# Second MLP product: five of seven block products in 512-column matmuls, six rotating PSUM banks per pair, half of the weight sums made by adding transfers

## The chip, the cores and the metric

The kernel runs on one core of one Trainium2 chip. The metric is the device time of one execution in microseconds; the median of three runs of the kernel before is 534.46 us (534.25 to 535.26).

## The reference

One transformer-like block on x of shape (2048 tokens, 512 channels), in fp32: linear attention with a softmax feature map (32 heads of 16) with its residual, giving h, and then a token-mixing MLP over h. The change is in the last product of the MLP:

```python
h2 = h + B(layernorm(h))
# B: layernorm again, then
u = gelu(einsum("bsd,sf->bdf", h, w1) + b1)     # F = 1792
y = einsum("bdf,fs->bds", u, w2) + b2           # back to S = 2048 tokens
return y.transpose                              # (S, D)
```

So the output rows of token t are h[t] plus the sum over f of w2[f, t] x u[:, f] plus b2[t].

## The kernel before, in words

A product of two fp32 matrices is made of three TensorE matmuls in float32r: each operand is split into a high part (a rounding copy by ScalarE) and a remainder (a subtraction), and high x high, high x remainder and remainder x high are added up in PSUM. `split` (L55 to L58) makes the two parts: the copy at L57 on ScalarE, the subtraction at L58 on the engine that is passed.

The first MLP product (`fill`, L622 to L635, with `mm3`, L60 to L64) runs 512-column matmuls; it fills PSUM tiles `pu`, and `gelu` (L723) writes u.

The second product (L763 to L847) takes the 1792 = 7 x 256 rows of w2 and the 2048 = 8 x 256 tokens in blocks of 256 x 256, and multiplies a block by a 2 x 2 scheme with seven block products in place of eight (Strassen's in Winograd's form). `operands_u` (L729) makes the seven combinations of u, each 128 x 256, once per p and keeps high part and remainder side by side in `UB[p, m]` (tiles `un` for p = 0 and 1, `uf` for the others). `STEPS` (L763) is 8 pairs of token tiles (sp) x 7 row blocks (p) = 56 steps. For every two steps (`GRP`), that is 28 groups, `stream_w2` (L767 to L781)

- loads four 128 x 128 blocks for each step into `wraw`, of which there are three, by two transfers of 256 KB on SP's queue (L773);
- makes the three further combinations, and one in place, by four VectorE operations of 256 columns (L777 to L780);
- splits all seven into `whi` and `wlo`, of which there are two each (L57 on ScalarE and L58 on VectorE, 1792 columns).

`product` (L787) runs three matmuls of 256 columns, L789: weights `whi` with the high part of u, `whi` with its remainder, `wlo` with the high part. `PROD` (L784) lists the seven products with the bank and the half of the bank that each adds into: seven halves of four banks per pair of token tiles. Even pairs use the four banks of `ps_b`, odd ones those of `ps_f` and `ps_q` (L806). The last step of a pair goes bank by bank (L813, L818); in the last pair the last two steps do (L834), so that the banks end one after the other.

A pair is drained by one ScalarE copy (L820), three VectorE sums (L821 to L823) and two operations of 512 columns that add b2 as well (L825). The result goes to the output, which holds h already, by two transfers of 256 KB that add in memory, issued by GpSimd (L827). The last pair has loaded its rows of h ahead (L832) and adds on VectorE (L836 to L846), then stores (L844, L847).

The order on the engines: up to the first product's middle it is written out by hand; in the stage of the second product a planner decides it from its own estimate of the times. It keeps program order as the priority, takes what is ready, and fixes the order of each engine's queue, which then runs in order on the chip. `issue_after` (L776) keeps the VectorE sums behind one instruction of the first product. A tile with n buffers is written again only when all readers of its earlier use are done.

Of the kernel before, what the change touches and what calls it, by code (L numbers as in the profile page):

```python
# [9 lines left out]
F32 = mybir.dt.float32  # L10
F32R = mybir.dt.float32r
AF = mybir.ActivationFunctionType
ALU = mybir.AluOpType
# [4 lines left out]
P = 128  # L18
S, D, H, DH, F = 2048, 512, 32, 16, 1792
NT = S // P  # L20
KD = D // P
NF = F // P
NG = 8
# [10 lines left out]
def block_kernel(ctx: ExitStack, tc: tile.TileContext, x, xT, wT, phic, wo, w1, b1, w2, b2,  # L34
                 kvmask, ident_in, out):
    nc = tc.nc
# [9 lines left out]
    b2s = cst.tile([P, NT], F32, name="b2s")  # L46
# [21 lines left out]
    ps_q = ctx.enter_context(tc.tile_pool(name="ps_q", bufs=2, space=PSUM, side="right"))  # L68
# [290 lines left out]
    q = {"mm": 0, "logits": 0, "exp": 0, "sum": 0}  # L359
# [39 lines left out]
    for t in range(3, NT - 1):  # L399
        if t + 2 < NT:  # L400
            raw = load_x(t + 2)
# [193 lines left out]
    w2v = w2.rearrange("(k p) s -> p k s", p=P)  # L595
# [114 lines left out]
    NP = NF // 2  # L710
    HD = D // 2
# [9 lines left out]
    U, UB, far = {}, {}, {}  # L721
# [42 lines left out]
    GRP = 2  # L764
    AW = {}

    def stream_w2(n):  # L767
        steps = STEPS[n:n + GRP]
        raw = ws.tile([P, GRP, 7, P], F32, name="wraw", bufs=3)
        wh_ = ws.tile([P, GRP, 7, P], F32R, name="whi")  # L770
        wl_ = ws.tile([P, GRP, 7, P], F32R, name="wlo")
        for i, (sp, p) in enumerate(steps):
            nc.sync.dma_start(raw[:, i, 0:4].rearrange("p (k i) s -> p k (i s)", k=2),  # L773
                              w2v[:, 2 * p:2 * p + 2, sp * 2 * P:(sp + 1) * 2 * P])
            AW[sp, p] = wh_[:, i], wl_[:, i]
        with tc.issue_after(LO[-18]):  # L776
            nc.vector.tensor_add(raw[:, :, 4], raw[:, :, 0], raw[:, :, 2])  # L777
            nc.vector.tensor_sub(raw[:, :, 0], raw[:, :, 1], raw[:, :, 0])
            nc.vector.tensor_sub(raw[:, :, 5], raw[:, :, 4], raw[:, :, 1])
            nc.vector.tensor_sub(raw[:, :, 6], raw[:, :, 3], raw[:, :, 5])  # L780
# [6 lines left out]
    def product(o, a, b, start, stop):  # L787
        for i, (x, y) in enumerate(((0, 0), (0, 1), (1, 0))):
            nc.tensor.matmul(o, a[x], b[:, y], start=start and i == 0, stop=stop and i == 2, skip_group_check=True)  # L789

    def products(sp, ps, order):
        for a, b, bk, half, opens in order:
            for p in ps:
                wh_, wl_ = AW[sp, p]
                product(bank[bk][:, half], (wh_[:, a], wl_[:, a]), UB[p, b], p == 0 and opens, p == NP - 1)

    def flat(a):
        return a.rearrange("p k d -> p (k d)")

    for n, (sp, p) in enumerate(STEPS):  # L800
# [12 lines left out]
        by_bank = sorted(PROD, key=lambda m: m[2:4])  # L813
# [3 lines left out]
        if not last:  # L817
            products(sp, [p], by_bank)  # L818
            ot = uo.tile([P, 2, 2, HD], F32, name="ot", bufs=1)
            nc.scalar.activation(e[:, 1], bank[0][:, 0], AF.Copy)  # L820
            nc.vector.tensor_add(u2, bank[0][:, 1], e[:, 1])  # L821
            nc.vector.tensor_add(u3, bank[1][:, 0], u2)
            nc.vector.tensor_add(e[:, 0], bank[2][:, 0], u2)  # L823
            for i, add in enumerate((u3.unsqueeze(1).to_broadcast([P, 2, HD]), e)):
                nc.vector.scalar_tensor_tensor(ot[:, i], bank[2 + i], b2s[:, t + i:t + i + 1], add,  # L825
                                               op0=ALU.add, op1=ALU.add)
                nc.gpsimd.dma_start(out[(t + i) * P:(t + i + 1) * P, :], flat(ot[:, i]), accum_op=ALU.add)  # L827
            continue
# [5 lines left out]
        products(sp, [p - 1, p], by_bank)  # L834
        nc.scalar.activation(e[:, 1], bank[0][:, 0], AF.Copy)
        nc.vector.tensor_add(hb[1][:, 1], bank[0][:, 0], hb[1][:, 1])  # L836
        nc.vector.tensor_add(u2, bank[0][:, 1], e[:, 1])
        nc.vector.tensor_add(hb[1][:, 0], u2, hb[1][:, 0])
        nc.vector.tensor_add(u3, bank[1][:, 0], u2)
        nc.vector.tensor_add(hb[0], hb[0], u3.unsqueeze(1).to_broadcast([P, 2, HD]))  # L840
        nc.vector.tensor_add(hb[0][:, 0], bank[2][:, 0], hb[0][:, 0])
        nc.vector.tensor_add(hb[1][:, 0], bank[2][:, 0], hb[1][:, 0])
        nc.vector.tensor_add(hb[0][:, 1], bank[2][:, 1], hb[0][:, 1])
        nc.sync.dma_start(out[t * P:(t + 1) * P, :], flat(hb[0]))  # L844
        for k, q in ((0, nc.scalar), (1, nc.sync)):
            nc.vector.tensor_add(hb[1][:, k], bank[3][:, k], hb[1][:, k])  # L846
            q.dma_start(out[(t + 1) * P:NT * P, k * HD:(k + 1) * HD], hb[1][:, k])  # L847


def _layout(A_x, A_wqkv, A_w_phi, A_wo, B_w1, B_b1, B_w2, B_b2):  # L850
# [7 lines left out]
    for a in range(P // DH):  # L858
# [3 lines left out]

    wo = np.asarray(A_wo).reshape(2, 4, 2, 32, D).transpose(2, 0, 1, 3, 4).reshape(D, D)
# [8 lines left out]
        "w2": np.asarray(B_w2),  # L872
# [22 lines left out]
```

## Time and profile before

| what | value |
|---|---|
| median of three runs | 534.46 us |
| span of the profiled execution, first to last instruction | 532.6 us |
| TensorE busy in the span | 520.8 us (98%), 3616 matmuls |
| VectorE, ScalarE, GpSimd busy | 384.4, 271.9, 234.8 us |
| second product, first to last matmul start | 385.8 to 526.8 us |
| its matmuls | 1176 of 256 columns |
| 256 KB weight load, issue to landing, median in the stage | 3.2 us |
| 256 KB adding transfer to the output, issue to landing, median | 4.8 us |

The profile has no time of its own for the execution it recorded beside the span; what lies around the span is not in it, and the median of the runs is 1.9 us above it. Times in rows of instructions are microseconds from the span's start. PE is TensorE's matmul side, PEld its weight loads, DVE VectorE, ACT ScalarE, POOL GpSimd, SP the queue that issues plain transfers. In a row of instructions the first number is the start, the second the time busy, and `x8` the number of instructions merged into the row; matmuls overlap in the pipeline, so their rate is read from their starts. What stands after `<-` in brackets ended the idle time before the row. A row of a window has the window, then busy time and count for PE, PEld, DVE, ACT and POOL, the granted clock, the busy share of the DMA engines and GB/s.

### The profile page before, as it was taken

The numbers are of one execution on the slowest core, as the hardware profiler recorded it, in microseconds if no ns is written. First come the engines' busy times: TensorE is split into PE (matmuls) and PEld (weight loads), VectorE is DVE, ScalarE is ACT, GpSimd is POOL, SyncE is SP. The second block draws the span as 40 slices with busy tenths as digits, with TensorE's granted clock in tenths as the row PEclk, the third lists the DMA queues.
The fourth block names the chain that finished last, engine by engine and source line by source line (L and its number), as shares of the span: only waits on it lengthen the run. The fifth ranks groups of instructions, "written<-read, shape, count | busy, mean of one in ns | idle before, by whom it ended". The sixth has DMA issues, their size and how long they took to land.

```text
span 532.6 us, 9386 instructions
## 1 busy us (share of the span) xinstructions
PE 520.8 (98%) x3616; PEld 448.7 (84%) x3616; DVE 384.4 (72%) x680; ACT 271.9 (51%) x460; POOL 234.8 (44%) x190
## 2 busy tenths in 40 slices
PE   8999999999999989999999999999999999999995
PEld 7888888886877767777788888888899999999995
DVE  6993999877699989875325524835668877887784
ACT  6998844424336776557746423525444243343340
POOL 2589699877889988887325000000001101100110
PEclk9999999999999999999999999999999999999999
DMA  8633310020502233334255333542014556535631
GB/s 309 206 110 118 99 22 21 1 72 9 160 0 79 82 101 116 104 116 136 85 176 159 98 100 98 159 117 82 20 41 107 143 148 153 123 120 136 143 75 46
DMA packets 45486, 55.81 MB, mean 105 GB/s; under 512 B 3969, under 2 KB 33025, under 8 KB 45441
## 3 DMA queue, kind: packets, MB, share of 16 engines
q1 hardware_dynamic: 43136, 51.38, 30.7%
q0 software_dynamic: 2016, 3.67, 5.5%
q8 instruction: 28, 0.46, 0.4%
q10 hardware_dynamic: 288, 0.17, 0.1%
q14 instruction: 18, 0.14, 0.1%
HBM read 46.81 MB, written 8.39 MB: 104 GB/s over the span
## 4 chain that ended last, share of the span: by engine, by line
PE 83%; POOL 9%; DVE 3%; ACT 2%; issue 1%; DVEq 0%; POOLq 0%; ACTq 0%
PE py L789 26%; PE pu L62 11%; PE pu L63 11%; PE pu L64 11%; POOL ez L442 4%; POOL eq L460 3%; PE pv L63 2%; PE pv L64 2%; PE pv L62 2%; PE pk_ps L62 2%; PE pk_ps L63 2%; PE pk_ps L64 2%; POOL hs L58 2%; PE po L62 1%; PE kvp L207 1%; PE po L63 1%
## 5 line engine op out<-in xcount | busy, mean ns | idle before, releaser
L827 POOL DMA_DIRECT2D out<-ot x14 | 12.5, 1001 | 212.2 <-DVE ot L825 212.2
L789 PE MATMUL py<-uf,whi 128*128 128x256 f32 x560 | 96.2, 283 | 0.0
L63 PE MATMUL pu<-hs,whi 128*128 128x512 f32 x224 | 87.6, 391 | 1.8 <-POOL hs L58 1.8
L602 DVE TENSOR_TENSOR wlo<-wraw,whi 128x512 fp32r<-128x512 f32 x56 | 50.3, 903 | 51.8 <-ACT whi L610 50.7
L57 ACT ACTIVATE whi<-wraw 128x1792 fp32r<-128x1792 f32 x28 | 47.7, 1705 | 77.9 <-PE py L789 73.8
L62 PE MATMUL pu<-hs,whi 128*128 128x512 f32 x224 | 87.4, 395 | 0.0
L64 PE MATMUL pu<-hs,wlo 128*128 128x512 f32 x224 | 87.2, 390 | 0.0
L789 PEld LDWEIGHTS py<-uf,whi 128*128 128x128 f32 x560 | 83.3, 192 | 0.0
L789 PE MATMUL py<-uf,wlo 128*128 128x256 f32 x280 | 69.9, 283 | 0.0
L58 DVE TENSOR_TENSOR wlo<-wraw,whi 128x1792 fp32r<-128x1792 f32 x28 | 56.6, 2022 | 15.4 <-ACT whi L57 15.4
L610 ACT ACTIVATE whi<-wraw 128x512 fp32r<-128x512 f32 x56 | 35.0, 627 | 47.0 <-PE pu L63 44.8
L63 PEld LDWEIGHTS pu<-hs,whi 128*128 128x128 f32 x224 | 42.1, 188 | 11.0 <-POOL hs L58 2.8
L62 PEld LDWEIGHTS pu<-hs,whi 128*128 128x128 f32 x224 | 42.0, 188 | 10.9 <-issue 2.5
L64 PEld LDWEIGHTS pu<-hs,wlo 128*128 128x128 f32 x224 | 42.0, 188 | 9.1 <-DVE wlo L602 0.4
L789 PEld LDWEIGHTS py<-uf,wlo 128*128 128x128 f32 x280 | 49.7, 192 | 0.0
L442 POOL TENSOR_TENSOR ez<-eq,zB 128x1024 f32<-128x1024 f32 x16 | 40.9, 2559 | 2.5 <-ACT zB L488 2.5
L789 PE MATMUL py<-un,whi 128*128 128x256 f32 x224 | 38.4, 283 | 0.0
L195 POOL TENSOR_TENSOR pk<-pk,sk 128x1024 f32<-128x1024 f32 x16 | 31.0, 1941 | 9.8 <-DVE sk L194 9.0
L460 POOL TENSOR_TENSOR eq<-eq,w 128x1024 f32<-128x1024 f32 x16 | 32.0, 1997 | 4.0 <-DVE w L457 4.0
L789 PEld LDWEIGHTS py<-un,whi 128*128 128x128 f32 x224 | 33.2, 192 | 0.1
L199 POOL TENSOR_TENSOR zacc<-zacc,pk 128x1024 f32<-128x1024 f32 x13 | 31.3, 2405 | 0.6
L58 POOL TENSOR_TENSOR hs<-hn,hs 128x512 fp32r<-128x512 f32 x16 | 21.4, 1340 | 17.5 <-ACT hs L57 15.6
(165 smaller groups left out, 1176.5 us busy)
## 6 DMA issues: line engine op xcount, KB each, us to landing
wraw<-in_w SPq DMA_DIRECT2D x112, 256.0 KB, 2.9
xraw<-in_xT SPq DMA_DIRECT2D x16, 256.0 KB, 3.1
xh<-in_x SPq DMA_DIRECT2D x16, 256.0 KB, 2.6
h<-in_x SPq DMA_DIRECT2D x16, 256.0 KB, 2.7
out<-h SPq DMA_DIRECT2D x16, 256.0 KB, 3.0
out<-ot POOLq DMA_DIRECT2D x14, 256.0 KB, 4.8
wraw<-in_wT SPq DMA_DIRECT2D x12, 256.0 KB, 5.0
wo<-in_wo SPq DMA_DIRECT2D x4, 256.0 KB, 3.6
```

The lines of the kernel that those rows point to most:

```text
L57: nc.scalar.activation(hi, src, AF.Copy)
L58: lo_engine.tensor_sub(lo, src, hi)
L62: nc.tensor.matmul(o, ah, bh, start=first, stop=False)
L63: nc.tensor.matmul(o, ah, bl, start=False, stop=False)
L64: nc.tensor.matmul(o, al, bh, start=False, stop=last)
L195: nc.gpsimd.tensor_mul(heads(PK[t]), heads(PK[t]), sk.unsqueeze(2).to_broadcast([P, 2 * H, DH]))
L199: nc.gpsimd.tensor_add(zacc, zacc, PK[t])
L442: nc.gpsimd.tensor_mul(EZ[t], EQ[t], zB)
L460: nc.gpsimd.tensor_mul(heads(EQ[t]), heads(EQ[t]), W[t].rearrange("p g c h -> p (g c h)").unsqueeze(2).to_broadcast([P, 2 * H, DH]))
L602: LO.append(nc.vector.tensor_sub(wl_, raw, wh_).ins)
L610: nc.scalar.activation(wh_, raw, AF.Copy)
L789: nc.tensor.matmul(o, a[x], b[:, y], start=start and i == 0, stop=stop and i == 2, skip_group_check=True)
```

## The change

- w2 is laid out on the host so that a group's four blocks lie together: [28, 128, 4, 256]. A group is loaded by one transfer of 512 KB and a second of 128 KB that puts the first block into slot 4 as well; then one transfer of 256 KB issued by GpSimd adds the second block onto slot 0 and the third onto slot 4. VectorE makes two sums per group in place of four. `wraw` has four buffers in place of three.
- The sums differ in sign from those before, so the draining subtracts in places.
- Five of the seven products have a bank of their own: one matmul of 512 columns (`whi` with the high part and the remainder of u side by side, into both halves) and one of 256 (`wlo` with the high part, into the first half). The two halves are added when the bank is drained. The other two products share a bank, one half each, in three matmuls as before. In the last pair (`LAST`) the last product is in three as well.
- A pair takes six banks, which rotate over all eight.
- In every pair the last two steps go together, product by product.
- The scratch memory for the descriptors of GpSimd's transfers is 8192 bytes in place of the default.

```diff
     def stream_w2(n):
-        steps = STEPS[n:n + GRP]
-        raw = ws.tile([P, GRP, 7, P], F32, name="wraw", bufs=3)
-        wh_ = ws.tile([P, GRP, 7, P], F32R, name="whi")
-        wl_ = ws.tile([P, GRP, 7, P], F32R, name="wlo")
-        for i, (sp, p) in enumerate(steps):
-            nc.sync.dma_start(raw[:, i, 0:4].rearrange("p (k i) s -> p k (i s)", k=2),
-                              w2v[:, 2 * p:2 * p + 2, sp * 2 * P:(sp + 1) * 2 * P])
-            AW[sp, p] = wh_[:, i], wl_[:, i]
+        g = n // GRP
+        raw = ws.tile([P, 7, GRP * P], F32, name="wraw", bufs=4)
+        wh_ = ws.tile([P, 7, GRP * P], F32R, name="whi")
+        wl_ = ws.tile([P, 7, GRP * P], F32R, name="wlo")
+        nc.sync.dma_start(raw[:, 0:4], w2[g])
+        nc.sync.dma_start(raw[:, 4], w2[g, :, 0])
+        nc.gpsimd.dma_start(raw[:, 0:5:4], w2[g, :, 1:3], accum_op=ALU.add)
+        for i, step in enumerate(STEPS[n:n + GRP]):
+            AW[step] = wh_[:, :, i * P:(i + 1) * P], wl_[:, :, i * P:(i + 1) * P]
         with tc.issue_after(LO[-18]):
-            nc.vector.tensor_add(raw[:, :, 4], raw[:, :, 0], raw[:, :, 2])
-            nc.vector.tensor_sub(raw[:, :, 0], raw[:, :, 1], raw[:, :, 0])
-            nc.vector.tensor_sub(raw[:, :, 5], raw[:, :, 4], raw[:, :, 1])
-            nc.vector.tensor_sub(raw[:, :, 6], raw[:, :, 3], raw[:, :, 5])
+            nc.vector.tensor_add(raw[:, 5], raw[:, 4], raw[:, 1])
+            nc.vector.tensor_add(raw[:, 6], raw[:, 3], raw[:, 5])
         split(wh_, wl_, raw, nc.vector)
...
-    PROD = ((1, 1, 0, 0, True), (2, 6, 2, 1, True), (3, 3, 3, 1, True), (4, 4, 2, 0, False), (0, 0, 1, 0, True),
-            (5, 5, 0, 1, False), (6, 2, 3, 0, False))
+    PROD = ((1, 1, 0, None), (5, 5, 1, None), (0, 0, 2, 0), (4, 4, 2, 1), (2, 6, 3, None), (6, 2, 4, None),
+            (3, 3, 5, None))
+    LAST = PROD[:-1] + ((3, 3, 5, 0),)
...
+        if half is None:
+            nc.tensor.matmul(o, a[0], b, start=start, stop=stop, skip_group_check=True)
+            nc.tensor.matmul(o[:, 0], a[1], b[:, 0], start=False, stop=stop, skip_group_check=True)
+            return
         for i, (x, y) in enumerate(((0, 0), (0, 1), (1, 0))):
...
-            pools = [ps_f, ps_f, ps_q, ps_q] if sp % 2 else [ps_b] * 4
-            bank = [pool.tile([P, 2, HD], F32, name="py", tag="pu") for pool in pools]
-        if p < NP - 1 - last:
-            products(sp, [p], PROD)
+            bank = []
+            for _ in range(6):
+                pool = (ps_f, ps_q, ps_b, ps_b)[n_bank % 8 // 2]
+                bank.append(pool.tile([P, 2, HD], F32, name="py", tag="pu"))
+                n_bank += 1
+        order = LAST if last else PROD
+        if p < NP - 2:
+            products(sp, [p], order)
             continue
         if p < NP - 1:
             continue
+        products(sp, [p - 1, p], order)
...
             nc.scalar.activation(e[:, 1], bank[0][:, 0], AF.Copy)
-            nc.vector.tensor_add(u2, bank[0][:, 1], e[:, 1])
-            nc.vector.tensor_add(u3, bank[1][:, 0], u2)
-            nc.vector.tensor_add(e[:, 0], bank[2][:, 0], u2)
...
+            nc.vector.tensor_add(e[:, 1], bank[0][:, 1], e[:, 1])
+            nc.vector.tensor_sub(u2, bank[1][:, 0], e[:, 1])
+            nc.vector.tensor_add(u2, bank[1][:, 1], u2)
+            nc.vector.tensor_sub(u3, u2, bank[2][:, 0])
+            nc.vector.scalar_tensor_tensor(e[:, 0], bank[2][:, 1], -1.0, u2, op0=ALU.mult, op1=ALU.subtract)
+
+            def out_block(i, h, o, add, low=None):
+                nc.vector.scalar_tensor_tensor(ot[:, i, h], o, b2s[:, t + i:t + i + 1], add, op0=ALU.add, op1=ALU.add)
+                if low is not None:
+                    nc.vector.tensor_add(ot[:, i, h], low, ot[:, i, h])
+
+            out_block(0, 0, bank[2][:, 1], u3)
+            out_block(0, 1, bank[3][:, 0], u3, bank[3][:, 1])
+            nc.gpsimd.dma_start(out[t * P:(t + 1) * P, :], flat(ot[:, 0]), accum_op=ALU.add)
+            out_block(1, 0, bank[4][:, 0], e[:, 0], bank[4][:, 1])
+            out_block(1, 1, bank[5][:, 0], e[:, 1], bank[5][:, 1])
+            nc.gpsimd.dma_start(out[(t + 1) * P:(t + 2) * P, :], flat(ot[:, 1]), accum_op=ALU.add)
             continue
...
-        for k, q in ((0, nc.scalar), (1, nc.sync)):
-            nc.vector.tensor_add(hb[1][:, k], bank[3][:, k], hb[1][:, k])
-            q.dma_start(out[(t + 1) * P:NT * P, k * HD:(k + 1) * HD], hb[1][:, k])
+        nc.vector.tensor_add(hb[1][:, 0], bank[4][:, 0], hb[1][:, 0])
+        nc.vector.tensor_add(hb[1][:, 0], bank[4][:, 1], hb[1][:, 0])
+        nc.scalar.dma_start(out[(t + 1) * P:NT * P, 0:HD], hb[1][:, 0])
+        nc.vector.tensor_add(hb[1][:, 1], bank[5][:, 0], hb[1][:, 1])
+        nc.sync.dma_start(out[(t + 1) * P:NT * P, HD:D], hb[1][:, 1])
...
-    nc = bacc.Bacc("TRN2", target_bir_lowering=False, num_devices=1)
+    nc = bacc.Bacc("TRN2", target_bir_lowering=False, num_devices=1, dynamic_dma_scratch_size=8192)
```

In the last pair the draining before has ten VectorE operations after the ScalarE copy (L836 to L846, one of them of 512 columns), and after the change fourteen.

More of the change, by code (lines that the diff above doesn't have):

```diff
@@ L22 @@
 NF = F // P
+NP = NF // 2
+HD = D // 2
+GRP = 2
 NG = 8
@@ L788, in product @@
         for i, (x, y) in enumerate(((0, 0), (0, 1), (1, 0))):
-            nc.tensor.matmul(o, a[x], b[:, y], start=start and i == 0, stop=stop and i == 2, skip_group_check=True)
+            nc.tensor.matmul(o[:, half], a[x], b[:, y], start=start and first and i == 0, stop=stop and i == 2,
+                             skip_group_check=True)
     def products(sp, ps, order):
-        for a, b, bk, half, opens in order:
+        for a, b, bk, half in order:
             for p in ps:
                 wh_, wl_ = AW[sp, p]
-                product(bank[bk][:, half], (wh_[:, a], wl_[:, a]), UB[p, b], p == 0 and opens, p == NP - 1)
+                product(bank[bk], half, (wh_[:, a], wl_[:, a]), UB[p, b], half != 1, p == 0, p == NP - 1)
@@ L797, in flat @@
     def flat(a):
         return a.rearrange("p k d -> p (k d)")
+    n_bank = 0
     for n, (sp, p) in enumerate(STEPS):
```

34 lines of the change are left out of this document (14 added, 20 removed).

## The prediction

> **What bounds the kernel now.** First the page: which engine the chain that ended last runs through, and at what clock. Then the windows of the stage that the diff touches (386 to 527 us), then its instructions.
>
> ```profile
> span 532.6 us, 9386 instructions
> PE 520.8 (98%) x3616; PEld 448.7 (84%) x3616; DVE 384.4 (72%) x680; ACT 271.9 (51%) x460; POOL 234.8 (44%) x190
> ...
> PE 83%; POOL 9%; DVE 3%; ACT 2%; issue 1%; DVEq 0%; POOLq 0%; ACTq 0%
> ```
> ```profile
> 406.00:426.00 20.00, 20.00 (x169) 20.00 (x168) 17.06 (x27) 7.21 (x5) 3.72 (x4) 1.00 0.61 138
> ```
> The reader sees TensorE (PE) busy throughout at the full granted clock (1.00), VectorE (DVE) 85% busy beside it, and the DMA engines a little over half. A busy PE says nothing of its rate, so I count starts.
>
> ```profile
> L789 PE MATMUL py<-uf,wlo x280: 279/283/283, 391.1 to 526.8; 128*128 128x256 f32 x140
> ...
> L789 PE MATMUL py<-un,whi x224: 278/283/283, 385.8 to 514.1; 128*128 128x256 f32 x112
> ```
> ```profile
> L63 PE MATMUL pu<-hs,whi x89: 389/389/389, 299.7 to 359.5; 128*128 128x512 f32 x89
> L64 PE MATMUL pu<-hs,wlo x89: 389/389/389, 299.9 to 359.8; 128*128 128x512 f32 x89
> L62 PE MATMUL pu<-hs,whi x89: 389/389/389, 300.2 to 360.0; 128*128 128x512 f32 x89
> ```
> The second product has 56 steps x 21 = 1176 matmuls of 256 columns. The first starts at 385.8, the last at 526.8: 141.0 us / 1175 = **120.0 ns each**, with no gap. The 512-column matmuls of the first product: 267 starts from 299.7 to 360.0, 60.3 / 266 = **226.7 ns each**. The 256 further columns cost 106.7 ns, so 13.3 ns of each matmul does not depend on its width.
>
> What feeds PE, and with how much room, is in the rows of one group (two steps) in order of time.
>
> ```profile
> 395.98 1.70 ACT L57 ACTIVATE whi<-wraw 128x1792 fp32r<-128x1792 f32 x1 [3.34 <-PE py L789]
> ```
> ```profile
> 397.72 2.03 DVE L58 TENSOR_TENSOR wlo<-wraw,whi 128x1792 fp32r<-128x1792 f32 x1 [3.02 <-ACT whi L57]
> 399.66 0.42 DVE L777 TENSOR_TENSOR wraw<-wraw 128x256 f32<-128x256 f32 x1
> 400.11 0.42 DVE L778 TENSOR_TENSOR wraw<-wraw 128x256 f32<-128x256 f32 x1
> 400.45 0.42 DVE L779 TENSOR_TENSOR wraw<-wraw 128x256 f32<-128x256 f32 x1
> 400.91 0.42 DVE L780 TENSOR_TENSOR wraw<-wraw 128x256 f32<-128x256 f32 x1
> 402.76 2.02 DVE L58 TENSOR_TENSOR wlo<-wraw,whi 128x1792 fp32r<-128x1792 f32 x1 [1.43 <-ACT whi L57]
> ```
> ```profile
> 400.94 1.12 PE L789 MATMUL py<-uf,whi 128*128 128x256 f32 x8
> ```
> ScalarE (ACT) waits until PE lets go of the weight buffer of two groups back (395.98), DVE makes the remainder (397.72 to 399.66, 1.94 us of its queue), and PE starts that group's high parts at 400.94; the planner puts eight of them ahead, so the first remainder is wanted at 400.94 + 8 x 0.12 = 401.9. The margin is 2.2 us, and the path that ends last is PE's own stream.
>
> **The change part by part, against the profiled span.**
>
> Wider matmuls. A step had 21 x 120 = 2520 ns. It now has five products of one 512- and one 256-column matmul (226.7 + 120 = 346.7 ns) and two of three: 5 x 346.7 + 6 x 120 = 2453 ns. Each merge saves 13.3 ns. There are 49 steps x 5 and, in the last pair (LAST keeps one product in thirds), 7 x 4: 273 merges x 13.3 = **-3.64 us**. The weight loads, one per matmul, go with them. The trace shows no stage that alternates the two widths. The ends are 0 (a merged matmul still takes 2 x 120) and -3.64: both widths carry the 13.3 ns, so no row allows a matmul under its columns plus that. I take the sum of the two rows, which are the nearest.
>
> Here a rule speaks against the change. The Trainium skill, "TensorE: Matmul & The Clock Gate", section "Back-to-back issue gap", puts the gap between matmuls at the columns over 2.4 GHz plus 2.5 ns. By it a merge would save 2.5 ns, 0.7 us in all; the trace's 120.0 and 226.7 ns disagree, as both have 13.3 ns beside their columns.
>
> Six banks per pair. A pair draws the next six of eight banks, so its first two are free and the other four are the first four of the pair before. With the last two steps taken product by product, those end 4.2, 3.5, 2.1 and 1.4 us before the pair's end, and the new pair reaches them 0.7, 1.4, 1.7 and 2.1 us after its start: 3.5 to 4.9 us for two to five DVE steps of some 0.34 us (the start-to-start of the sums above), with at most one remainder of 1.94 ahead. I cost it at nothing; the cover is that room.
>
> Both steps at once. In even pairs (0, 2, 4, 6) steps 5 and 6 lie in two groups, so one group is wanted 2.45 us earlier and the other let go 2.1 us later. From release to remainder is 1.7 + 0.05 + 1.94 = 3.7 us, against 2.45 + 0.35 us of other work: written strictly, 0.9 us of waiting, twice in four pairs, **7 us**. But the row at 400.94 shows the planner putting high parts first, 1.6 us of them in a new step, which covers 0.9. I take 0 and keep 7 for the range.
>
> DVE. Two sums per group go, 3.5 x 2 x 0.42 = 2.9 us a pair; draining takes 12 operations of 256 (5.0 us) where it took
>
> ```profile
> L821 DVE TENSOR_TENSOR u<-py,e x7: 416/417/418, 405.0 to 511.4; 128x256 f32<-128x256 f32 x7
> ...
> L825 DVE SCALAR_TENSOR_TENSOR ot<-py,b2s,u x7: 743/745/747, 407.0 to 513.4; 128x512 f32<-128x512 f32 x7
> ```
> three of 0.417 and two of 0.743 (2.7 us). DVE falls by 0.6 us a pair, off the path: nothing.
>
> Adding transfers. The queues' rows for 386 to 533 us, and transfers alone and in company (SP's are the weight loads, POOL's the adding ones to the output):
>
> ```profile
> wraw<-in_w SPq DMA_DIRECT2D x46, 256.0 KB, 3.2
> out<-ot POOLq DMA_DIRECT2D x14, 256.0 KB, 4.8
> ```
> ```profile
> 410.00:411.00 1.00, 1.00 (x10) 1.00 (x10) 0.97 (x3) 0.00 (x0) 0.07 (x1) 1.00 0.89 141
> 416.00:417.00 1.00, 1.00 (x10) 1.00 (x10) 0.56 (x2) 0.81 (x1) 0.00 (x0) 1.00 0.85 285
> ```
> From 410 to 411 only an adding transfer runs: 141 GB/s at a share of 0.89, 158 at a full one. From 416 to 417 only loads: 285 / 0.85 = 335. A group now loads 640 KB (655 kB / 335 = 1.96 us), adds 256 KB (262 / 158 = 1.66) and bears 2/3.5 of an output block (0.95): **4.6 us of 4.91**. It fits, narrowly. The adding transfer's pieces are 1 KB where the output's are 2 KB: if its time went by pieces it would be 3.3 us, the sum 6.2; if adding into SBUF cost what a load does, 0.8 and 3.7. I take 4.6.
>
> Latency. The chain for a raw buffer is now: remainder done, load, adding transfer, two sums.
>
> ```profile
> DMA to landing us min/median/max: 2.5/2.8/3.0
> ```
> ```profile
> DMA to landing us min/median/max: 6.5/6.7/6.8
> ```
> ```profile
> DMA to landing us min/median/max: 4.0/5.3/6.6
> ```
> ```profile
> DVE wraw L777 <- DMA wraw<-in_w: 11.5, 7, 3.3
> ```
> The first is two loads alone (issued at 394.7 and 395.2; the pair is in after 3.5 us), the second two loads behind an output pair (496.6), the third that pair on POOL's queue (408.1). So L, from remainder to landed sum, is about 3.5 + 0.4 for the further 128 KB + 4.0 = 7.9 us undisturbed, and up to 13 behind output blocks. Four raw buffers allow 4 x 4.91 - 1.7 - 2 = 15.9 us: hidden, **0**, provided DVE's queue does not wait on it early (second rival). Behind the adding transfer on POOL's queue wait only output blocks, whose buffer is next wanted a pair (17 us) later; POOL computes nothing here.
>
> The end.
>
> ```profile
> 526.82 0.28 PE L789 MATMUL py<-uf,wlo 128*128 128x256 f32 x1
> ```
> ```profile
> 524.26 0.39 ACT L835 ACTIVATE e<-py 128x256 f32<-128x256 f32 x1 [5.57 <-PE py L789]
> ```
> ```profile
> 528.06 0.75 DVE L846 TENSOR_TENSOR hb<-py,hb 128x256 f32<-128x256 f32 x2
> ```
> The end is DVE's: ten operations after the copy at 524.26, done at 528.81, 1.9 us after PE's last start + 0.12. Now there are 14, four more at 0.34 to 0.45: +1.4 to +1.8 us; but the first bank is complete 4.2 us before PE's end instead of 3.6, and the last one needs one operation, not two. I take **+0.6**, between -0.5 and +1.5.
>
> Sum: -3.64 + 0.6 = **-3.0 us** on a span of 532.6. The median of the runs, 534.46, lies 1.9 us over the span; I carry that over: **531.4 us**.
>
> **The rivals.**
>
> The fixed part doesn't fall (or two or three of the hidden waits eat it): merges save 0.7, the end takes 0.6, **534.3**. Against it: two widths with the same 13.3 ns. Chance 0.07.
>
> Late sums in DVE's queue, slower. DVE runs in order, and in the rows above the sums of a coming group stand right behind one remainder and ahead of the next. If the planner leaves group g+4's sums ahead of the remainder of g+2, the loop remainder, load, adding, sums, remainder takes L + 0.67 + 1.94 + 0.1 for two groups. It decides from L = 2 x 4.91 - 2.7 = 7.1 us on. At L = 7.9 a group takes 5.3 us, at 9.5 it takes 6.1; from the sixth group on (22 of them) that is +9 to +26 us, in the middle +18, **549**. For it: the 7 waits of L777 on a landing, up to 3.3 us, which were harmless only because L was 3.5 to 7. Against it: a planner that expects so late a landing puts the sums one remainder later, where 12 us are allowed. Chance 0.22.
>
> The DMA engines become the bound: by pieces, 6.2 us a group, +1.3 x 22 = +29, **560**. The Trainium skill, "DMA: Bandwidth & Descriptors", section "Queues, rings and completion order", says each engine takes turns between queues packet by packet; the 6.7 us landing agrees. Chance 0.06.
>
> Double groups wait as written: +7 less what the high parts cover, +3 to +7, **534 to 538**. Chance 0.08.
>
> **How the numbers follow.** Forecast as summed: 0.57; own range 529.9 to 533. The range reaches down to 529.5 (the end at its best, -0.5, gives 530.3, and 0.8 us, 0.15%, is left for the measurement), and up to 547: it holds the forecast, no change, the double groups and the lower part of the late sums (+9 to +13), some 0.57 + 0.07 + 0.08 + 0.08, and leaves 0.2 out, all of it above. A measurement here tells about 0.2% (1.1 us) from no change. Faster 0.57, within 0.2% 0.07, slower 0.36.
>
> **What would show it.** Right: starts in the stage at 346.7 ns per merged product, PE without idle time from 386 to about 523 us, and L58's waits on ACT alone. Late sums: L778's successors wait on a landing in most groups and PE waits on L58. DMA bound: a share near 1 throughout and landings that grow. Double groups: PE waits at each second pair's end only. A stage of 141 us without waits would refute the 13.3 ns.

## The result, and the profile after

The changed kernel takes **590.63 us** (median of four runs, 587.52 to 591.90) against 534.43 us before (four runs, 534.25 to 535.26): a ratio of 1.104 with a 95% interval of 1.101 to 1.107. The prediction was 531.4 us in a range up to 547. Its sign was wrong, and the time lies 59 us above it, 44 above the range.

The page of the changed kernel, its first line, its engines and its chain:

```profile
span 588.8 us, 8941 instructions
...
PE 540.3 (92%) x3343; PEld 446.3 (76%) x3343; DVE 380.2 (65%) x677; ACT 270.6 (46%) x460; POOL 267.9 (46%) x218
...
PE 60%; DMA 14%; DVE 9%; POOL 9%; ACT 4%; issue 3%; SPq 0%; POOLq 0%; DVEq 0%; ACTq 0%
```

The 273 matmuls that the merges were to save are gone (3616 to 3343), but PE's share of the chain fell from 83 to 60% and DMA, which had none, has 14%. VectorE is less busy than before, in a longer span, and PE fills less of its span: no engine became a bound by its load. The stage itself, first and last matmul:

```profile
L792 PE MATMUL py<-uf,wlo x85: 277/283/415, 391.9 to 582.5; 128*128 128x256 f32 x85
...
L788 PE MATMUL py<-un,whi x78: 387/398/767, 386.0 to 569.0; 128*128 128x512 f32 x78
```

It lasts 582.5 - 386.0 = 196.5 us where it was 141.0: the whole loss lies in it. The maxima (415 and 767 ns beside medians of 283 and 398) tell of matmuls at a lower clock. The window that was shown of before:

```profile
406.00:426.00 20.00, 17.53 (x87) 14.72 (x87) 11.86 (x21) 4.99 (x3) 4.19 (x4) 0.83 0.65 145
```

PE is without work for 2.5 of 20 us and its granted clock is 0.83; VectorE is busy for 11.9 us in place of 17.1; the DMA engines are at 0.65. All have time to spare, so something waits for something in a circle. Three of the longest waits in the stage:

```profile
ACT whi L60 <- PE py L788: 104.1, 14, 15.0
...
DVE wraw L777 <- DMA wraw<-in_w: 32.9, 13, 5.6
...
PE py L788 <- DVE u L831: 20.0, 7, 4.9
```

Total, times and the longest, in us. VectorE's first sum (L777) waits for a landing 13 times; PE waits up to 4.9 us for L831, which is a *draining* operation and not a weight. In order of time on VectorE (L61 is the remainder, L777 and L778 the sums, L829 to L836 the draining; line numbers have moved by some from before):

```profile
392.75 2.03 DVE L61 TENSOR_TENSOR wlo<-wraw,whi 128x1792 fp32r<-128x1792 f32 x1 [1.60 <-ACT whi L60]
397.72 2.03 DVE L61 TENSOR_TENSOR wlo<-wraw,whi 128x1792 fp32r<-128x1792 f32 x1 [2.95 <-ACT whi L60]
405.31 0.43 DVE L777 TENSOR_TENSOR wraw<-wraw 128x256 f32<-128x256 f32 x1 [5.57 <-DMA wraw<-in_w]
405.77 0.42 DVE L778 TENSOR_TENSOR wraw<-wraw 128x256 f32<-128x256 f32 x1
406.12 0.42 DVE L829 TENSOR_TENSOR e<-py,e 128x256 f32<-128x256 f32 x1
408.70 2.02 DVE L61 TENSOR_TENSOR wlo<-wraw,whi 128x1792 fp32r<-128x1792 f32 x1
```

The remainder at 392.75 ends at 394.78 and lets a raw buffer go; its next content is summed at 405.31. That is the loop's L, **10.5 us** where I had 7.9. For the last 5.57 us VectorE stands still, and behind it stand the draining of the first pair and the next remainder, which starts at 408.70, 11 us after the one before. (Its copy on ScalarE ran from 403.12 to 404.82, so its data were there 3.9 us before.) The row that groups the stage's remainders:

```profile
L61 DVE TENSOR_TENSOR wlo<-wraw,whi x26: 2011/2019/2026, 392.7 to 573.8; 128x1792 fp32r<-128x1792 f32 x26
```

26 of them from 392.7 to 573.8 are 181.1 / 25 = 7.24 us for each group, where the prediction's products ask 4.91.

Thirty microseconds on, the chain of the same kernel (start, length, what) and PE's two rows:

```profile
428.07 7.24 DMA wraw<-in_w
...
435.33 0.06 DVE wraw L777
...
435.67 0.42 DVE wraw L778
436.09 0.40 DVE ot L836
436.49 0.34 DVE u L831
...
436.96 0.77 PE py L788
```
```profile
431.80 0.28 PE L792 MATMUL py<-un,wlo 128*128 128x256 f32 x1
...
436.96 0.77 PE L788 MATMUL py<-un,whi 128*128 128x512 f32 x1 [4.88 <-DVE u L831]
```

An adding transfer lands at 435.31; two sums, then two draining operations, then PE, which has waited 4.88 us for a PSUM bank. The draining had nothing to do with the transfer; it only stood behind the sums in VectorE's queue. And the clock after such a wait, by windows:

```profile
431.00:432.00 1.00, 1.00 (x10) 0.88 (x8) 0.44 (x2) 0.00 (x0) 0.00 (x0) 1.00 0.77 255
432.00:437.00 5.00, 0.12 (x2) 0.07 (x1) 1.67 (x5) 0.00 (x0) 1.20 (x1) 0.81 0.48 77
437.00:440.00 3.00, 3.00 (x9) 2.39 (x9) 3.00 (x6) 0.00 (x0) 0.00 (x0) 0.50 0.47 69
440.00:443.00 3.00, 3.00 (x16) 2.78 (x16) 2.58 (x8) 0.00 (x0) 0.78 (x2) 0.68 0.63 207
```

The granted clock is 1.00 before the wait, 0.81 across it, 0.50 for the 3 us after it and 0.68 in the next 3. Taken as stretches of full and half clock, half clock begins 1.9 us before 437 and ends 1.9 us after 440: PE works at half clock for 4.9 us after its wait. The Trainium skill, "TensorE: Matmul & The Clock Gate", section "What's actually happening", says that an idle window of about 3.4 us brings the clock to half and a busy one brings it back; these rows agree. Start to start, 29 steps between matmuls are over 0.45 us, 46.7 us in all; beyond a usual step of 0.235 us each, that is 40 of the 55.5 us that the stage grew by. The rest is lower clock and smaller gaps. How much the lower clock costs by itself is not known, since PE waits for its feed anyway.

### The profile page after: what moved, and what is told of

Same layout as the page of the kernel before. It is cut to its first block, busy times and chain, and to the rows that moved or that the text cites. A ratio compares the mean times of both kernels' runs of the same rounds, so it can differ in the third digit from the quotient of the medians.

```text
span 588.8 us, 8941 instructions
## 1 busy us (share of the span) xinstructions
PE 540.3 (92%) x3343; PEld 446.3 (76%) x3343; DVE 380.2 (65%) x677; ACT 270.6 (46%) x460; POOL 267.9 (46%) x218
## 4 chain that ended last, share of the span: by engine, by line
PE 60%; DMA 14%; DVE 9%; POOL 9%; ACT 4%; issue 3%; SPq 0%; POOLq 0%; DVEq 0%; ACTq 0%
DMA wraw<-in_w 13%; PE pu L65 10%; PE pu L67 10%; PE pu L66 10%; PE py L788 4%; DVE wlo L61 4%; POOL ez L445 3%; PE py L792 2%; PE py L789 2%; POOL eq L463 2%; PE pv L66 2%; PE pv L67 2%; PE pv L65 2%; PE pk_ps L65 2%; ACT whi L60 2%
## 5 line engine op out<-in xcount | busy, mean ns | idle before, releaser
L773 POOL DMA_DIRECT2D wraw<-in_w x28 | 34.5, 1231 | 190.9 <-DMA wraw<-in_w 173.9
L60 ACT ACTIVATE whi<-wraw 128x1792 fp32r<-128x1792 f32 x28 | 46.7, 1696 | 115.7 <-PE py L788 104.1
L61 DVE TENSOR_TENSOR wlo<-wraw,whi 128x1792 fp32r<-128x1792 f32 x28 | 56.4, 2021 | 46.0 <-ACT whi L60 46.0
L788 PE MATMUL py<-uf,whi 128*128 128x512 f32 x195 | 72.2, 423 | 6.9 <-ACT whi L60 6.9
L789 PE MATMUL py<-uf,wlo 128*128 128x256 f32 x195 | 49.4, 297 | 1.6 <-DVE wlo L61 1.6
L788 PE MATMUL py<-un,whi 128*128 128x512 f32 x78 | 32.2, 450 | 20.0 <-DVE u L831 20.0
L788 PEld LDWEIGHTS py<-uf,whi 128*128 128x128 f32 x195 | 36.9, 204 | 13.3 <-ACT whi L60 9.0
L789 PEld LDWEIGHTS py<-uf,wlo 128*128 128x128 f32 x195 | 36.9, 202 | 5.8 <-DVE wlo L61 4.3
L777 DVE TENSOR_TENSOR wraw<-wraw 128x256 f32<-128x256 f32 x28 | 11.5, 421 | 38.2 <-DMA wraw<-in_w 38.1
L792 PE MATMUL py<-uf,whi 128*128 128x256 f32 x170 | 35.4, 298 | 0.0
L788 PEld LDWEIGHTS py<-un,whi 128*128 128x128 f32 x78 | 15.4, 208 | 25.2 <-issue 21.2
```

Of the source, the lines that this page charges most:

```text
L60: nc.scalar.activation(hi, src, AF.Copy)
L61: lo_engine.tensor_sub(lo, src, hi)
L788: nc.tensor.matmul(o, a[0], b, start=start, stop=stop, skip_group_check=True)
L789: nc.tensor.matmul(o[:, 0], a[1], b[:, 0], start=False, stop=stop, skip_group_check=True)
L792: nc.tensor.matmul(o[:, half], a[x], b[:, y], start=start and first and i == 0, stop=stop and i == 2, skip_group_check=True)
```

## The experiments

The theory from this profile is the second rival of the prediction: **sums late in VectorE's queue** (A). Against it stand, from the start, that the DMA engines are at their limit, that the wide products with six banks wait on something of their own (F), that both last steps together do it (D), and that VectorE has too much to do in the wrong moment (E1). A and F can both hold. Each ratio is against the kernel before, run beside it on the same chip.

### Holding the sums back: e1_sums_after_two and e1b_sums_after_one

`issue_after` keeps the sums of group g behind the remainder of group g - 2, or g - 1, in VectorE's queue:

```diff
+    REM = []
-        with tc.issue_after(LO[-18]):
+        with tc.issue_after(REM[g - 2] if g >= 4 else LO[-18]):   # e1b: REM[g - 1]
...
-        split(wh_, wl_, raw, nc.vector)
+        nc.scalar.activation(wh_, raw, AF.Copy)
+        REM.append(nc.vector.tensor_sub(wl_, raw, wh_).ins)
```

> The changed kernel, with the two VectorE sums of group g held in VectorE's queue behind the remainder of group g-2, one remainder later than most of them stood. Theory A (VectorE runs in order and stands at sums whose adding transfer has not landed, with draining and remainders behind them): the loop now has three groups for about 10.5 + 2.7 us, 4.4 us each, under PE's 4.9, so most of the loss goes: 531 to 540 us. Theory B (the adding transfers themselves bring the weights too slowly, whatever the order): still 565 us or more. Theory C (six banks or both steps at once make PE wait): still 565 us or more.

> As the run before, with the sums of group g behind the remainder of group g-1, the latest place that still comes before their own high part. Theory A: room for a landing is 4 x 4.9 - 6.5 = 13 us, so 531 to 540 us, but ScalarE's copy now waits on sums made just before it, which may cost some tenths of a us per group. Theory B and C: 565 us or more.

Measured: 560.18 us behind g - 2 (ratio 1.046, 1.042 to 1.050) and 552.94 behind g - 1 (1.033, 1.031 to 1.035). Moving two instructions of 0.42 us of each group is worth 30.4 us and 37.7 us, with the same transfers, the same sums and the same products. 18 us of loss stay. Both times lie above the 531 to 540 us expected of A alone, and below the 565 us of B and C: A is a large part of the loss, not all of it.

The planner orders every queue anew, so PE's order can move as well. PE's rows tell it by the tiles of u (`un` for p = 0 and 1, `uf` for the rest). Behind g - 2 it stays nearly that of the changed kernel: pairs 2 and 6 still open with 24 matmuls of one group, then 24 of the next, then the rest of the first. Behind g - 1 these pairs open with the first group's 32 matmuls in a row. So some 30 us go with the sums' place alone, and the further 7 us are not separated from PE's order.

### Without the adding transfers: e2_no_adding

One load of 512 KB, and all four sums on VectorE, as before the change; product, banks and draining as after it:

```diff
-        nc.sync.dma_start(raw[:, 4], w2[g, :, 0])
-        nc.gpsimd.dma_start(raw[:, 0:5:4], w2[g, :, 1:3], accum_op=ALU.add)
...
+            nc.vector.tensor_add(raw[:, 4], raw[:, 0], raw[:, 2])
+            nc.vector.tensor_add(raw[:, 0], raw[:, 0], raw[:, 1])
```

> The changed kernel without adding transfers: one load of 512 KB per group and all four sums on VectorE; wide matmuls, six banks and both steps at once stay. Theory A and B: 530 to 533 us, the 3.6 us of the merged matmuls less what the end costs. Theory C: PE still waits on banks at each pair's end, 550 us or more. If the fixed 13.3 ns of a matmul does not fall with the merge: 534 to 535 us.

Measured: 557.15 us (1.041, 1.039 to 1.043). The other half of the change, alone, loses 22 us in place of gaining 3. So there is a second cause, and it has nothing to do with adding transfers. Two rows of its waits:

```profile
ACT whi L60 <- PE py L788: 74.1, 14, 9.2
...
PEld py L789 <- DVE wlo L61: 12.8, 16, 1.6
```

### The adding transfers alone: e3_adding_only, and e8_adding_only_late

The product of before (1176 matmuls of 256 columns, four banks, the old draining but for the sums' signs) with the changed weight path and layout; e8 also holds the sums behind the remainder of g - 1, as e1b does.

```diff
-        raw = ws.tile([P, GRP, 7, P], F32, name="wraw", bufs=3)
+        raw = ws.tile([P, 7, GRP * P], F32, name="wraw", bufs=4)
...
+        nc.sync.dma_start(raw[:, 0:4], w2[g])
+        nc.sync.dma_start(raw[:, 4], w2[g, :, 0])
+        nc.gpsimd.dma_start(raw[:, 0:5:4], w2[g, :, 1:3], accum_op=ALU.add)
...
-        with tc.issue_after(LO[-18]):
+        with tc.issue_after(REM[g - 1] if g >= 4 else LO[-18]):   # e8 alone
```

> The kernel before (three matmuls of 256, four banks, alternating) with the adding transfers, the new layout of w2 and four raw buffers. Theory A: the sums again stand ahead of a remainder that cannot wait, 545 to 590 us, a little less than the changed kernel as there are fewer drains. Theory B: the same. Theory C: 534 to 537 us.

> The kernel before with adding transfers (the run e3_adding_only, 577.9 us), and the two VectorE sums of group g held behind the remainder of group g-1. Theory A (only the sums' place in VectorE's queue makes the adding transfers dear): 534 to 540 us, as the old product has four banks at a time and no late drains. If the transfers' volume is dear by itself: 560 us or more.

Measured: e3 577.90 us (1.080, 1.075 to 1.085), e8 534.43 us (ten runs; 0.999, 0.998 to 1.000). The waits of e3, and then the rows of e8 that hold its first and its last matmul:

```profile
DVE wraw L777 <- DMA wraw<-in_w: 75.5, 18, 7.6
PEld py L787 <- DVE wlo L61: 35.3, 13, 5.4
PE py L787 <- DVE wlo L61: 32.7, 13, 5.2
```
```profile
L789 PE MATMUL py<-uf,wlo x280: 279/283/283, 391.1 to 526.8; 128*128 128x256 f32 x140
...
L789 PE MATMUL py<-un,whi x224: 278/283/283, 385.9 to 514.1; 128*128 128x256 f32 x112
```

In e3 VectorE waits 75.5 us for landings and PE then for the remainder. With the sums moved in the queue the stage ends at 526.8, where it ended before the change: +43 us becomes nothing. PE's order is nearly the same in e3 and e8. That settles A, and it refutes the DMA engines as the bound, since e8 moves the same bytes by the same transfers in 141 us.

### What in the other half loses 22 us: e4_sums_gpsimd, e5_no_drain, e6_even_last_step

All three start from e2. e4 gives the two further sums to GpSimd (`nc.vector` to `nc.gpsimd`), so that VectorE has no more of them than after the change. e5 leaves out the draining of the first seven pairs. e6 takes the last two steps together only in odd pairs. In this order:

```diff
-            nc.vector.tensor_add(raw[:, 4], raw[:, 0], raw[:, 2])
-            nc.vector.tensor_add(raw[:, 0], raw[:, 0], raw[:, 1])
+            nc.gpsimd.tensor_add(raw[:, 4], raw[:, 0], raw[:, 2])
+            nc.gpsimd.tensor_add(raw[:, 0], raw[:, 0], raw[:, 1])
```
```diff
         if not last:
-            ot = uo.tile([P, 2, 2, HD], F32, name="ot", bufs=1)
-            nc.scalar.activation(e[:, 1], bank[0][:, 0], AF.Copy)
...
-            nc.gpsimd.dma_start(out[(t + 1) * P:(t + 2) * P, :], flat(ot[:, 1]), accum_op=ALU.add)
             continue
```
```diff
-        if p < NP - 2:
+        both = last or sp % 2 == 1
+        if p < NP - 1 - both:
...
-        products(sp, [p - 1, p], order)
+        products(sp, [p - 1, p] if both else [p], order)
```

> The kernel without adding transfers (557.2 us), with two of the four sums on GpSimd instead of VectorE; two weight buffers, six banks. VectorE's work falls by 3.5 x 2 x 0.335 = 2.3 us of some 16 us a pair. Theory E1 (drains are late because VectorE has too much to do): at most 545 us. Theory E2 (drains are late because the last two steps' products wait for the second group's remainder, and the held weight buffers pass that on): 550 us or more.

> The kernel without adding transfers (wide matmuls, six banks, both steps at once, four sums on VectorE), with the draining of the first seven pairs left out: their part of the second product does not reach the output. It measures PE's stream by itself. If a merged product takes 226.7 + 120 ns: the stage starts at 386 to 388 us and its last matmul 137.4 us later, 531 us in all. If merging saves 2.5 ns only: 140.3 us, 534 us. Theory D (in even pairs the last two steps hold both weight buffers, whatever the draining does): PE still waits once or twice in each even pair, 3 to 10 us more. Theory E (drains that come late keep banks from the next pair): no waits.

> The kernel without adding transfers, but in even pairs, whose last two steps lie in two groups, only the last step goes product by product; odd pairs as they are. Theory D: the second group is wanted at its own step again, so most of the 22 us go: 533 to 540 us. Theory E: banks now end later in even pairs, so it is not better than 555 us.

Measured: e4 560.26 us (1.048, 1.046 to 1.050), no better than e2: VectorE's load is not it. e6 557.84 us (1.043, 1.040 to 1.045), no better: both steps together are not it either, at least not alone. e5 533.09 us, one execution beside a median of 534.85: without the draining, which frees the banks and also takes its work from VectorE and its transfers from the DMA engines, the loss is gone. A row of its matmuls, and its longest waits from 386 us on, on ScalarE and VectorE:

```profile
L792 PE MATMUL py<-uf,wlo x85: 278/283/287, 392.7 to 525.2; 128*128 128x256 f32 x85
```
```profile
ACT whi L60 <- PE py L788: 56.5, 20, 3.3
DVE wlo L61 <- ACT whi L60: 28.2, 21, 3.5
```

No row of its waits has PE waiting in the stage, though steps are taken together in every pair and two weight buffers serve them. So the loss hangs on the draining; yet PE's own waits in e2 are mostly for weights:

```profile
PE py L789 <- DVE wlo L61: 7.7, 12, 1.3
PE py L788 <- ACT whi L60: 6.0, 7, 1.0
PE py L792 <- DVE e L829: 2.3, 2, 1.3
PE py L788 <- DVE u L831: 0.3, 1, 0.3
```

Only the last two rows, 2.6 us, are waits for a bank in draining (L829, L831). The link is the order of PE's queue, which the planner wrote. Here each entry is a group's number, from 0, and how many of its matmuls stand in a row (a step with two groups' weights open has several short runs):

```text
e2   ... 3x14 4x4 3x2 4x20 3x2 4x4 3x2 4x4 5x32 6x32 7x24 8x24 7x4 8x4 7x4 8x4 ...
e5   ... 3x20 4x32 5x32 ...
```

In e2, 24 matmuls of group 8 stand ahead of the last ones of group 7. Group 7 is the first of pair 2, and group 3 holds the first step of pair 1: both meet a pair whose banks are still in part in draining. Read from the order, the planner puts the products on those banks off and draws the following group's ahead. The changed kernel's PE rows have the same order at these places. Group 7's weights stay in use until the last of its products, and there are only two buffers. On ScalarE, which fills them, this is seen as:

```profile
413.23 3.29 ACT L60 ACTIVATE whi<-wraw 128x1792 fp32r<-128x1792 f32 x2 [7.35 <-PE py L788]
...
436.62 3.29 ACT L60 ACTIVATE whi<-wraw 128x1792 fp32r<-128x1792 f32 x2 [9.19 <-PE py L788]
```

It waits for PE for 7 to 9 us, then two groups' copies come back to back, their remainders follow late, and PE waits for those.

### More weight buffers, fewer banks: e7, e9, e10, e11

If that is so, either a third buffer for `whi` and `wlo` or a bank less per pair should take the loss back. e7 is e2 with three buffers of each (and, for room, three raw buffers and 2048 bytes of descriptor scratch); e9 has the two sums on GpSimd besides. e10 is e7 with three wide products in place of five, so with five banks and two draining operations less; e11 is the same with the buffers and the scratch of e2. The first cut is e7's, the second that of e10 and e11.

```diff
-        raw = ws.tile([P, 7, GRP * P], F32, name="wraw", bufs=4)
-        wh_ = ws.tile([P, 7, GRP * P], F32R, name="whi")
-        wl_ = ws.tile([P, 7, GRP * P], F32R, name="wlo")
+        raw = ws.tile([P, 7, GRP * P], F32, name="wraw", bufs=3)
+        wh_ = ws.tile([P, 7, GRP * P], F32R, name="whi", bufs=3)
+        wl_ = ws.tile([P, 7, GRP * P], F32R, name="wlo", bufs=3)
```
```diff
-    PROD = ((1, 1, 0, None), (5, 5, 1, None), (0, 0, 2, 0), (4, 4, 2, 1), (2, 6, 3, None), (6, 2, 4, None),
-            (3, 3, 5, None))
+    PROD = ((1, 1, 0, None), (5, 5, 1, None), (0, 0, 2, 0), (4, 4, 2, 1), (2, 6, 3, 0), (6, 2, 3, 1),
+            (3, 3, 4, None))
...
-            for _ in range(6):
+            for _ in range(5):
```

> The kernel without adding transfers, with three whi and three wlo buffers in place of two (three raw buffers in place of four, and less descriptor scratch, to make room); order of products unchanged. Theory D: a group held for longer no longer keeps the next from being split: 531 to 536 us. Theory E: PE still waits on banks at each pair's end, 545 us or more.

> Three weight buffers (542.5 us) and two of the four sums on GpSimd. Theory E1 and E2 both: less than 542; if both the buffers and VectorE's work have room, 533 to 536 us, the limit that the run without draining showed (533.1 us).

> Three weight buffers and four sums on VectorE (542.5 us), but three wide products instead of five and five banks per pair, so that the next pair finds three of its banks free instead of two, and two drain operations fewer. If late banks are what is left of the loss: 534 to 538 us; the merged matmuls then bring 3/5 of what five bring. If not: 540 us or more.

> The kernel without adding transfers (557.2 us with six banks) with three wide products and five banks per pair; weight buffers stay at two. In PE's planned order no group's last products stand any more among the next group's. Theory F (with six banks the planner puts off the products whose bank is still being drained, their group's weights are let go a group late, and ScalarE and VectorE split the next group late): with the order mended two buffers are enough, 532 to 536 us. Theory G (two weight buffers are too few for both steps at once, whatever the banks): 540 us or more, and only the third buffer explains the 532.7 us of five banks.

Measured: e7 542.45 us (1.014, 1.012 to 1.016), e9 540.71 (1.011, 1.008 to 1.013), **e10 532.67** (ten runs, 532.02 to 534.86; 0.996, 0.995 to 0.998), e11 538.64 (1.007, 1.006 to 1.009). Of e2's 22.3 us the third buffer takes back 14.7, going to five banks 18.5, both together all and 2 more. e7 and e11 each lie between the two times forecast for them, so neither the buffer nor the banks are the whole cure. e9, with less work on VectorE, is only 1.7 us below e7, and not at the 533 to 536 us expected if that work were what was left. e10 is faster than both kernels, by 0.4% of the one before. The page of e10's profiled execution, which was its slowest:

```profile
span 533.1 us, 9043 instructions
...
PE 520.4 (98%) x3455; PEld 440.5 (83%) x3455; DVE 392.2 (74%) x717; ACT 271.5 (51%) x460; POOL 234.8 (44%) x190
```

In e11, with two weight buffers, all that is left of waits on PE's side is this:

```profile
PEld py L789 <- DVE wlo L61: 6.0, 4, 1.7
```
```profile
406.69 0.39 PE L788 MATMUL py<-un,whi 128*128 128x512 f32 x1
408.14 0.51 PE L789 MATMUL py<-un,wlo 128*128 128x256 f32 x2 [1.06 <-DVE wlo L61]
```
```profile
406.07 2.02 DVE L61 TENSOR_TENSOR wlo<-wraw,whi 128x1792 fp32r<-128x1792 f32 x1
```

Four waits, each where an even pair (0, 2, 4, 6) hands over to the next; the first is from 406.69 to 408.14, 1.45 us, and ends with the remainder that starts at 406.07. That is the fourth rival, double groups, by its mechanism: a remainder that comes late where both steps of an even pair went together. Its size was 7 us by the strict count, 0.9 us twice in each of four pairs; measured are 6, some 1.5 us once in each, so that the totals are close is partly luck. It was hidden in the larger loss until the banks were fewer, and the third buffer removes it (in e10 PE waits 1.4 us in all, for banks).

### Everything at once: e12_five_banks_adding_late

The changed kernel with its sums held behind g - 1 (e1b) and with five banks, two weight buffers:

> The changed kernel (590.6 us) with two edits: the sums of group g held behind the remainder of g-1, and three wide products on five banks. Theories A and F together name the whole loss, so both edits together give 531 to 536 us. If adding transfers and rotating banks cost something together that neither shows alone: 540 us or more.

Measured: 544.81 us (1.019, 1.017 to 1.021). The edit is e1b's together with e10's `PROD`, banks and draining. Both cures on the whole change leave 10 us. Two of its longest waits:

```profile
ACT whi L780 <- DVE wraw L779: 62.8, 17, 5.0
DVE wlo L781 <- ACT whi L780: 35.8, 19, 3.0
```

Held so late, the sums stand right before ScalarE's copy, which now waits for them 17 times, and the copy before the remainder: copy and remainder run in a row after each sum, with no group's lead. In ScalarE's rows these copies start at 426.96, 431.68 and 436.39, 4.7 us apart, where PE's products ask about 5; from the copy at 420.22 to that at 426.96, with a pair's draining on VectorE between, it is 6.7. So this loop has little room, and a pair's draining does not fit into it. e8 bore the same without loss, with fewer draining operations and no pair whose last two steps, taken together, lie in two groups. PE's starts have ten steps over 0.45 us: four of 1.6 to 1.7 us where an even pair hands over to the next, as in e11, and six of 0.6 to 1.0 us behind the hand-over of odd pairs. Beyond a usual step of 0.235 us these are 5.8 and 3.4 us. The forecast of 531 to 536 us was missed, as it took the two cures to name the whole loss. A version with adding transfers, late sums and three weight buffers was not run.

## Why the prediction was wrong, point by point

**The failed step** is "Four raw buffers allow 4 x 4.91 - 1.7 - 2 = 15.9 us: hidden, 0, provided DVE's queue does not wait on it early". The proviso is what failed. The rival had the mechanism right: group g + 4's sums stand ahead of the remainder of g + 2, as the rows from 397.72 to 408.70 show. I gave it 0.22, on the ground that a planner that expects so late a landing puts the sums later. It did not: VectorE waits for a landing 13 times in the stage. And it is not only the remainder that is late, as I had written: the draining stands behind the sums too, and PE's longest waits are for banks. The sums moved back show what that costs: 43 us without the wide products (e3 to e8), and with them 30 (e1) to 38 (e1b, in which PE's order moved too).

**L was mis-sized**, 7.9 in place of 10.5 us. I had taken the adding transfer by a row of a transfer into the output (4.0 us at the least) and the loads undisturbed. Measured, in the changed kernel's first group:

```profile
398.86 1.20 POOL L773 DMA_DIRECT2D wraw<-in_w  x1 [53.68 <-DMA wraw<-in_w]
```
```profile
DMA to landing us min/median/max: 6.4/6.4/6.4
```
```profile
DMA to landing us min/median/max: 5.0/5.2/5.4
```

The adding transfer issued at 398.86 needs 6.4 us where the sum had 4.0: that is 2.4 of the 2.6 us. Its own group's loads, from 394.80 on, were through 4.1 us after the remainder's end, where 3.9 were forecast. The next group's two loads, issued beside the adding transfer at 399.8 and 400.2, need 5.0 and 5.4. Over the whole kernel the median is this, against the 4.8 of the adding output transfers that I had shown:

```profile
wraw<-in_w POOLq DMA_DIRECT2D x28, 256.0 KB, 5.4
```

By the prediction's own formula, two groups for each L + 0.67 + 1.94 + 0.1, an L of 10.5 gives 6.6 us a group and 22 x 1.7 = +37 us, where the 7.9 had given 9. From remainder to remainder e3 takes 6.78 us, with a loss of 43, and the changed kernel 7.24, so the formula is somewhat low. That e1b gave back nearly the same (37.7) is partly chance: the second loss lies in the same loop, and PE's order moved.

**"Six banks per pair ... I cost it at nothing"** is the second failed step, and no rival stood for it. The room that I counted, 3.5 to 4.9 us, took VectorE to be at the draining at once, with at most one remainder ahead. On the chip it is not. These are the first and the last step of pair 0's draining in e2:

```profile
404.55 0.42 DVE L829 TENSOR_TENSOR e<-py,e 128x256 f32<-128x256 f32 x1
...
411.04 0.75 DVE L838 TENSOR_TENSOR ot<-py,ot 128x256 f32<-128x256 f32 x2
```

It takes 7.2 us, because sums of a coming group and a remainder stand between its steps; the new pair starts at 404.81 (but for two matmuls drawn ahead) and, by the prediction's count, wants its last bank 2.1 us later, at 406.9. So banks are late. PE nevertheless waits little for them (2.6 us in e2), because the products that want them stand later in its queue. That is what I had not asked: what the *planner* does when it thinks that a bank is late. It reorders PE, and the reordering holds two weight buffers for a group longer. The result is +22 us instead of -3.

Shown are the loss (e2), that it goes without draining (e5), that two thirds of it go with a buffer more (e7), more with one bank less (e11, which also has two wide products and two draining operations less), and all with both (e10), and the order itself. That the planner's estimate of the draining is the reason for its choice is read from that order, not measured by itself; no run held PE's order fixed with six banks and two buffers.

**The wide matmuls** do less than -3.64 us. In e5, where PE waits for nothing, the stage begins so:

```profile
387.00 0.28 PE L789 MATMUL py<-un,wlo 128*128 128x256 f32 x1
387.12 0.40 PE L788 MATMUL py<-un,whi 128*128 128x512 f32 x1
```

902 of the 903 matmuls run from 387.00 to 525.22 (one was pulled ahead); with one more step of 0.24 us that is 138.5 us against 141.0: 2.5 us saved, 9 ns a merge in place of 13.3. The term was right in sign, but its size was not: 1.1 us of the 3.64 were not there. The 2.5 ns of the Trainium skill ("TensorE: Matmul & The Clock Gate", section "Back-to-back issue gap") are further off than the row was; that section gives them for an isolated matmul and says that weight loads count too in a stream of both, which the prediction left out. Even with all waits gone the change's products are worth 0.5% of the kernel at most.

**The DMA engines as the bound** is refuted by e8, and by the share of 0.65 above. **VectorE's load**, costed at nothing, was no cause: with less of it e4 is not faster than e2. **Double groups** cost 6 us for the 7 written, in half as many waits of more length, and are seen by themselves only where the larger loss is gone. **The end** was +0.6: from the last matmul's start to the span's end it is 588.8 - 582.5 = 6.3 us after and 532.6 - 526.8 = 5.8 before, +0.5.

The losses do not add: 43 (e3) and 22 (e2) make 65, the change loses 56. A likely reason, not tested by itself, is that both hold ScalarE, VectorE and PE in the same loop, and who waits for the slower of two does not wait for both.

## What to carry to other kernels

An instruction that waits for a transfer costs what stands behind it in its queue, not its own 0.4 us: before a cheap operation gets a longer-lived source, look up its neighbours in the engine's order, and work out the loop by the latency measured in company of the other transfers, not alone. Where a planner orders the work, a resource that it believes late (a bank in draining) is paid in another one (weight buffers held by products drawn ahead), so cost a rotation by what the order then holds open. And test each half of a double change alone: here each lost by itself, for reasons of its own, and one of them was mended by moving two instructions.

## What the hardware showed that I had not expected

- Adding takes about twice as long for each piece: in the packet records of the changed kernel a piece of 1 KB added into SBUF takes 102 ns and one of 2 KB added into the output 178, where plain ones take 46 and 84 (medians). One adding transfer alone, between 400.5 and 402 in the changed kernel, starts no packet for about 1 us after its first ones. Yet its volume cost nothing in e8.
- A merged matmul of 512 columns followed by one of 256 starts the next 235 ns later in e5 (median), not 226.7, while from one of 256 to a wide one it is 118 in place of 120.0.
- A wait of PE of 4.9 us is followed by 4.9 us at half clock, so that a long wait can be paid for again in the matmuls behind it, unless PE has to wait again anyway.
